# Six attention chunks, 32 feed-forward steps and all weight conversions of a fused kernel in one fixed order

## The chip, the cores and the metric

The kernel runs on one core of a Trainium2 chip, as one program. The metric is the device time of that program in microseconds (us). TensorE is written PE below, VectorE DVE, ScalarE ACT, GpSimd POOL, and SyncE, which starts the transfers, SP. A core has one queue of instructions for each engine; every queue runs in its own order, and an instruction that waits for another engine holds up all that stands behind it in its queue.

## What is computed

Three layers follow each other. The reference, cut to what matters:

```python
# attention: batch 2, heads 8, seq 768, head_dim 40, float32
for t in range(S):
    m_new = np.maximum(f_gate[:, :, t] + m, i_gate[:, :, t])
    f_stab = np.exp(f_gate[:, :, t] + m - m_new)
    i_stab = np.exp(i_gate[:, :, t] - m_new)
    m = m_new
    C = f_stab * C + i_stab * outer(vt, kt)
    n = f_stab * n + i_stab * kt
    y[:, :, t] = sigmoid(o_gate[:, :, t]) * (C @ qt) / max(|n . qt|, 1.0)
# feed-forward: 1536 tokens, d_model 320, d_ff 2048, weights in float64
h = x @ w_in
x = (np.maximum(0.01 * h, h) @ w_out).astype(np.float32)
# 8 experts, dense, d_ff 1024; P is a gate made doubly stochastic in 8 rounds
for e in range(E):
    out += P[:, e:e + 1] * (np.maximum(x @ w1[e], 0.0) @ w2[e])
```

The weights `w_in` and `w_out` are float64: a random float32 array times a float64 scale. The kernel gets them as raw 64-bit words and makes float32 out of them on the chip.

## The kernel before

**Numbers.** Every float32 factor of a large product is split into a high part, in the fp32r format that PE multiplies, and a low part, the residue. A product is then three passes: high by high, high by low, low by high.

**Attention.** The recurrence is worked in chunks of 128 positions of one batch, 12 in all (6 positions times 2 batches, `Chunk`). For a chunk PE makes the decay exponents from `stt` and `bd` (`decay`, L450; `bd` comes from `spread`, L441), ACT takes the exponential (L451) into `Dm`, POOL cuts it to the causal half with an affine_select (L452). PE makes the scores of the heads (`scores`, L460), DVE multiplies them with `Dm` into `Pm` (`weigh`, L466), POOL makes weighted keys `kw` (L473). PE multiplies `Pm` with the values (L478), recalls the state carried from earlier chunks (`zps`, L482) and makes the new state. DVE scales and adds (L496, L498), finds the denominator (L501 to L503), POOL multiplies the sigmoid gate with it (L507), DVE multiplies the result with that (L508). PE transposes it, ACT and DVE split it into the high and low input of the feed-forward layer, `xT` (`split_x`, L285 to L287). `gates` makes the running maxima and sums on DVE, and splits them.

**Feed-forward.** Tokens go in 6 blocks of 256, two chunks each; the 2048 hidden units go in 16 slices of 128. A step is one slice of one block, 96 in all. `up(g)` makes 8 matmuls of 128x256 (`mm1`, L165) into a PSUM bank `ha`, of which there are two; ACT applies the leaky ReLU from there into an SBUF tile `gg` (L558) and copies its high part `hha` (L561); the low part `hla` (L562) is a subtraction in POOL, and for the six steps in `V_STEPS` in DVE. `down(g)` adds 2 x 3 matmuls of 128x320 (`mm2`, L172 to L174) to the output banks `ya`, three steps after `up`. Steps run over block 0's first half, all of block 1, block 0's second half, and then block after block; block 0's two halves are added on DVE.

**Weights.** They come in 16 pieces, for each of 8 units one of `w_in` (768 columns in three rows of 256) and one of `w_out` (640). A piece is loaded on SP (`load`), ACT scales the upper word into a tile `up` and takes the top bits of the exponent (`prepare`, L127 and L130), DVE puts the sign in (L147) and joins the words to a float32 (L151), ACT copies the high part (L155), and POOL or, for the pieces of `V_PIECES`, DVE makes the low part (L156). Seven pieces of `HALVES` go through DVE in two halves.

**Order.** Up to the fourth piece chunks 0 and 1, the gates and the first conversions stand in an order written by hand (inside `tc.manual_schedule()`). After that the program is written step by step, with the rest hung ahead of and behind steps: `ATTEND` says at which steps the parts of a chunk come, `PIECES` at which steps a piece is converted. The framework's scheduler then places the instructions on the engines, by what is ready in its own estimate. Six chunks and all 16 pieces are placed by the time that step 32, the first of block 2, begins.

**Expert stage.** From 299.7 us on, eight experts run from their own hand-written order. It begins with the copies of its input, `X` (L222 to L229), which start during the last feed-forward steps.

## Time and profile before

| what | value |
|---|---|
| median of 3 runs | 968.94 us (968.02 to 975.64) |
| span of the profiled execution | 971.4 us |
| PE busy | 949.0 us, 98% |
| DVE busy | 575.3 us, 59% |
| ACT busy | 496.1 us, 51% |
| POOL busy | 608.8 us, 63% |
| start of the experts | 299.7 us |

Shares are averages over stages with different limits. The page's picture of the span in 40 slices, of 24.3 us each, shows where they differ: PE's row begins with 8 and 7 tenths and is then at 9 nearly throughout, and the clock that PE was granted is at 7, 5, 7, 9, 7 tenths in the first five slices and at 9 tenths or more behind them:

```
PE   8799999999999999999999999999999999999998
DVE  6769515142485658656666666566666666666655
ACT  5657444434466454555545455454454544545442
POOL 3354444644376656676777767777777677777762
PEclk7579799999999999999999999999999999999999
```

A busy PE at half clock does half the work of one at full clock, so both rows have to be read together.

### The profile page before, as it was taken

The page shows a single profiled execution, that of the slowest core. Times are in us where ns is not written, and L with a number is a line of the kernel's source. Part 1 is how long each engine was busy: PE and PEld are TensorE (multiplying, and loading weights), DVE is VectorE, ACT ScalarE, POOL GpSimd, SP SyncE. Part 2 cuts the span into 40 slices and gives each one's busy share as a digit, 9 for nine tenths or more (in the row PEclk, how much of TensorE's full clock was granted, in tenths as well). Part 3 has the DMA queues.
Part 4 walks back from the last instruction along what each step waited for, and adds up shares of the span by engine and source line. Part 5 has one row for each costly group of instructions (what it writes and reads, how often), then busy time and mean ns, then how long its engine had stood idle before and what let it go on. Part 6 is the DMA issues. An engine that isn't in the chain of part 4 may idle for free.

```text
span 971.4 us, 16851 instructions
## 1 busy us (share of the span) xinstructions
PE 949.0 (98%) x6174; PEld 920.4 (95%) x6174; DVE 575.3 (59%) x1121; ACT 496.1 (51%) x969; POOL 608.8 (63%) x618
## 2 busy tenths in 40 slices
PE   8799999999999999999999999999999999999998
PEld 6589898999989899999999999999999999999998
DVE  6769515142485658656666666566666666666655
ACT  5657444434466454555545455454454544545442
POOL 3354644444376656676777767777777677777762
PEclk7579799999999999999999999999999999999999
DMA  7545403010020111111111111111111111111102
GB/s 271 161 142 161 127 16 116 29 54 23 16 71 15 45 32 38 39 49 36 37 41 52 50 37 37 36 55 42 46 37 36 48 46 49 37 36 45 40 1 82
DMA packets 57161, 56.63 MB, mean 58 GB/s; under 512 B 7559, under 2 KB 47671, under 8 KB 57079
## 3 DMA queue, kind: packets, MB, share of 16 engines
q1 hardware_dynamic: 57078, 55.56, 18.8%
q8 instruction: 48, 0.79, 0.3%
q14 instruction: 35, 0.28, 0.1%
HBM read 53.57 MB, written 1.97 MB: 57 GB/s over the span
## 4 chain that ended last, share of the span: by engine, by line
PE 85%; DVE 4%; DMA 3%; ACT 2%; issue 2%; POOL 2%; SPq 1%; DVEq 0%; ACTq 0%; POOLq 0%
PE y L172 12%; PE y L173 11%; PE y L174 11%; PE b L881 8%; PE b L884 8%; PE b L882 8%; PE b L883 8%; PE ha L165 6%; PE ya L172 2%; PE yps L478 2%; PE ya L174 2%; DMA raw_a<-in_w_in_dram 2%; PE ya L173 2%; PE sps L460 1%; DMA R<-in_og_dram 1%
## 5 line engine op out<-in xcount | busy, mean ns | idle before, releaser
L903 POOL TENSOR_TENSOR hl<-c,hh 128x384 fp32r<-128x384 f32 x192 | 196.5, 1024 | 169.4 <-ACT c L902 148.2
L172 PE MATMUL y<-w_e,hh 128*128 128x320 f32 x768 | 238.1, 310 | 0.6 <-ACT acc L950 0.6
L173 PE MATMUL y<-w_e,hh 128*128 128x320 f32 x768 | 236.9, 308 | 0.0
L174 PE MATMUL y<-w_e,hl 128*128 128x320 f32 x768 | 236.8, 308 | 0.0
L954 DVE SCALAR_TENSOR_TENSOR acc<-y,Pg,acc 128x320 f32<-128x320 f32 x336 | 179.3, 548 | 63.4 <-PE y L174 56.3
L901 ACT ACTIVATE hh<-c 128x384 fp32r<-128x384 f32 x192 | 99.8, 520 | 207.4 <-DVE c L900 207.3
L881 PE MATMUL b<-X,w_e 128*128 128x384 f32 x448 | 152.9, 341 | 2.1 <-DVE s L912 1.5
L884 PE MATMUL b<-X,w_e 96*128 96x384 f32 x448 | 151.2, 337 | 0.0
L882 PE MATMUL b<-X,w_e 128*128 128x384 f32 x448 | 151.0, 337 | 0.0
L883 PE MATMUL b<-X,w_e 128*128 128x384 f32 x448 | 150.7, 336 | 0.0
L172 PEld LDWEIGHTS y<-w_e,hh 128*128 128x128 f32 x768 | 144.2, 188 | 1.9 <-ACT acc L950 1.0
L173 PEld LDWEIGHTS y<-w_e,hh 128*128 128x128 f32 x768 | 144.3, 188 | 0.0
L174 PEld LDWEIGHTS y<-w_e,hl 128*128 128x128 f32 x768 | 144.1, 188 | 0.0
L562 POOL TENSOR_TENSOR hla<-gg,hha 128x256 fp32r<-128x256 f32 x90 | 72.0, 802 | 96.9 <-ACT hha L561 84.5
L165 PE MATMUL ha<-xT,w_a 128*128 128x256 f32 x768 | 114.5, 292 | 3.7 <-ACT gg L558 2.5
L165 PEld LDWEIGHTS ha<-xT,w_a 128*128 128x128 f32 x768 | 103.4, 195 | 9.1 <-ACT gg L558 3.8
L902 ACT ACTIVATE c<-c 128x384 f32<-128x384 f32 x192 | 101.0, 526 | 17.8 <-ACT hh L901 0.7
L900 DVE TENSOR_TENSOR c<-b,s 128x384 f32<-128x384 f32 x192 | 100.7, 551 | 13.1 <-PE b L884 8.6
L919 DVE SCALAR_TENSOR_TENSOR hl<-b,hh 128x384 fp32r<-128x384 f32 x64 | 35.7, 558 | 94.7 <-ACT hh L918 94.6
L881 PEld LDWEIGHTS b<-X,w_e 128*128 128x128 f32 x448 | 84.8, 189 | 3.3 <-DVE s L912 2.2
L201 POOL TENSOR_TENSOR raw_e<-raw_e 128x256 f32<-128x256 f32 x116 | 84.4, 737 | 4.6
L882 PEld LDWEIGHTS b<-X,w_e 128*128 128x128 f32 x448 | 85.2, 190 | 0.0
(165 smaller groups left out, 1548.6 us busy)
## 6 DMA issues: line engine op xcount, KB each, us to landing
raw_e<-in_w_dram SPq DMA_DIRECT2D x32, 320.0 KB, 2.9
raw_e<-in_w_dram SPq DMA_DIRECT2D x62, 128.0 KB, 2.2
raw_e<-in_w_dram SPq DMA_DIRECT2D x248, 32.0 KB, 1.9
raw_a<-in_w_in_dram SPq DMA_DIRECT2D x8, 768.0 KB, 5.6
raw_a<-in_w_out_dram SPq DMA_DIRECT2D x8, 640.0 KB, 4.3
R<-in_kp_dram SPq DMA_DIRECT2D x11, 256.0 KB, 3.5
R<-in_qp_dram SPq DMA_DIRECT2D x11, 256.0 KB, 4.1
R<-in_vn_dram SPq DMA_DIRECT2D x11, 184.5 KB, 2.5
```

Of the source, the lines that this page charges most:

```text
L165: nc.tensor.matmul(h_ps, t1[:, ws, c * P:(c + 1) * P], xt[:, xs, t0:t0 + n], start=(j == 0), stop=(j == len(MM1) - 1),)
L172: nc.tensor.matmul(y_ps, a, t2[:, c, :], start=first, stop=False)
L173: nc.tensor.matmul(y_ps, a, t2[:, 2 + c, :], start=False, stop=False)
L174: nc.tensor.matmul(y_ps, b, t2[:, c, :], start=False, stop=last)
L881: nc.tensor.matmul(bank, f[:, 0], b[:, 0], start=fresh, stop=False, skip_group_check=not fresh)
L882: nc.tensor.matmul(bank, f[:, 0], b[:, 2], start=False, stop=False, skip_group_check=not fresh)
L883: nc.tensor.matmul(bank, f[:, 2], b[:, 0], start=False, stop=False, skip_group_check=not fresh)
L884: nc.tensor.matmul(bank, f[0:K3, 1], b[0:K3, 1], start=False, stop=True, skip_group_check=not fresh)
L900: nc.vector.tensor_tensor(c, part, plus, op=ALU.add)
L902: nc.scalar.activation(c, c, AF.Relu)
L903: nc.gpsimd.tensor_tensor(hl[a][b], c, hh[a][b].bitcast(F32), op=ALU.subtract)
L954: nc.vector.scalar_tensor_tensor(out=o, in0=y, scalar=Pg[:, 2 * HP * q + t, e:e + 1], in1=o, op0=ALU.mult, op1=ALU.add)
```

## The change

- **One table.** `ORDER` names everything that is done up to step 31's residue, in the order in which it is written to the queues, all inside `tc.manual_schedule()`: six chunks with their loads (`c0.kP` to `c5.xl`), the three parts of the gates (`a0` to `a8`, `n0` to `n8`, `f0` to `f8`), the 16 weight pieces (`L` load, `pu` scale, `pl` bits, `pa` sign, `pb` join, `ph` high, `px` low) and 32 feed-forward steps (`u` up, `g` leak, `h` high, `l` low, `d` down, `e` empty the output banks). `ATTEND`'s first rows, `PIECES`, `V_PIECES` and `V_STEPS` go.
- **Steps.** `RUNS` sets the first 32: block 0's slices 0 to 5, block 1's 0 to 9, block 0's 6 to 13, block 1's 10 to 15, block 0's 14 and 15. A block that is interrupted is summed through SBUF, so there are three such additions of two halves each, where there was one.
- **Leak in place.** `leak` writes the leaky values back into their PSUM bank, `inner_high` and `inner_low` read them there. `inner_low` is always on DVE. The tile `gg` is gone. This holds for all 96 steps.
- **Causal mask.** For chunks 0 to 3 a matmul of the identity with a mask of large negative numbers (bf16) adds the mask to the exponents in PSUM, two of 128x512 for a chunk; the affine_select is left for the later chunks.
- **Moved products.** In the table DVE makes the weighted keys, the gates with the denominator, the spreads and the weights' low parts, but for the eight in `POOLED`, which stay on POOL.
- **Weights.** No halves; the scale is written in place, so `up` goes, and its tile `rawU` becomes a fourth buffer of raw pieces.
- **Small things.** Reset flags and the mask are made by POOL's memsets at the start, the gates are loaded in three parts, the scores of chunks 0 and 1 use the feed-forward layer's banks, chunk 6 is loaded behind the table, its spread and one part of the decays come a little later.

From step 32 on the framework's scheduler places the instructions as before.

```diff
+RUNS = ((0, 0, 6), (1, 0, 10), (0, 6, 14), (1, 10, 16), (0, 14, 16))
+MASKED = (0, 1, 2, 3)
+POOLED = ('c0.kw', 'c1.kw', 'c4.kw', 'c4.sg', 'c5.sg', 'px14', 'px8', 'px9')
+ORDER = """
...
+px4 pl5 px3 pu6 L8 d0 c2.ya pu5 L7 c2.dn u2 c4.v pl6 c2.sg c2.ou c3.sc g2 c3.zt h2 pa5 l2 c2.tt pb5 u3 c2.xi c3.wg ph5
+u4 g3 px5 pu8 c3.va c2.xl g4 L9 pl8 pa6 h3 d1 c3.ya h4 pl7 c3.dn d2 l3 pu7 c3.sg u5 c3.ou pb6 c3.tt g5 c4.ap0 l4 c3.xi
...
-                self.up[p] = rawU[:, p * 3 * UW:p * 3 * UW + n]
-                nc.scalar.activation(self.up[p], self.raw[p][:, :, 1].bitcast(F32), AF.Copy, scale=F64_SCALE)
+                hw = self.raw[p][:, :, 1].bitcast(F32)
+                nc.scalar.activation(hw, hw, AF.Copy, scale=F64_SCALE)
...
+                nc.vector.scalar_tensor_tensor(out=hw, in0=hw, scalar=3, in1=lw, op0=ALU.logical_shift_left, op1=ALU.bitwise_or)
...
+        def low(self, p, eng):
+            t, n = self.t[p], (3, 2)[p]
+            eng.tensor_tensor(t[:, n:2 * n], self.value(p), t[:, 0:n].bitcast(F32), op=ALU.subtract)
...
+                nc.tensor.matmul(aps, stt[rs, s0:s0 + P], self.bd[rs, 4 * i:4 * i + 4, :], start=True, stop=not self.masked)
+                if self.masked:
+                    nc.tensor.matmul(aps, identb, mask.unsqueeze(1).to_broadcast([P, 4, P]), start=False, stop=True)
...
-            h_ps = ps_h.tile([P, BA], F32, tag="h", name=f"ha{g}")
-            mm1(h_ps, unitsA[f // 2].t[0], f % 2, xTb[j], 0, BA)
-            gg = ha.tile([P, BA], F32, tag="gg", name=f"gg{g}", bufs=4)
-            nc.scalar.activation(gg, h_ps, AF.Prelu, alpha=0.01)
+            h_ps[g] = ps_h.tile([P, BA], F32, tag="h", name=f"ha{g}")
+            mm1(h_ps[g], unitsA[f // 2].t[0], f % 2, xTb[j], 0, BA)
...
+        def leak(g):
+            nc.scalar.activation(h_ps[g], h_ps[g], AF.Prelu, alpha=0.01)
...
+        def inner_high(g):
             hh = ha.tile([P, BA], F32R, tag="hh", name=f"hha{g}")
             hl = ha.tile([P, BA], F32R, tag="hl", name=f"hla{g}")
-            nc.scalar.activation(hh, gg, AF.Copy)
-            (nc.vector if g in V_STEPS else nc.gpsimd).tensor_tensor(hl, gg, hh.bitcast(F32), op=ALU.subtract)
+            nc.scalar.activation(hh, h_ps[g], AF.Copy)
...
+        def inner_low(g):
+            hh, hl = hs[g]
+            nc.vector.tensor_tensor(hl, h_ps.pop(g), hh.bitcast(F32), op=ALU.subtract)
...
+        with tc.manual_schedule():
+            for name in ORDER.split():
+                tasks[name]()
+        chunks[6].load()
+        chunks[6].load_rest()
+        for g in range(TABLE, NG + LAG):
             if g < NG:
                 up(g)
+                leak(g)
+                inner_high(g)
+                inner_low(g)
             for fn in before[g]:
                 fn()
-            if g >= LAG:
-                down(g - LAG)
+            down(g - LAG)
+            empty(g - LAG)
```

Rows of the engines' queues follow, at three places: line, operation, target and sources (`w1` and `w2` are the converted pieces of a unit `a0` to `a7`, `raw` what they are made of, `R0` any of the chunks' tiles), and how many in a row.

First, DVE in the middle of the part. Before, between the residues of steps 14 and 15 and the scores of chunk 4 (`sps`):

```order
L562 TENSOR_TENSOR hla14_857<-gg14_854,hha14_856 128x256
L151 SCALAR_TENSOR_TENSOR raw0_a6_775<-rawU_94,raw0_a6_775 128x384 x2
L147 SCALAR_TENSOR_TENSOR raw1_a6_843<-raw1_a6_843 128x640
L562 TENSOR_TENSOR hla15_878<-gg15_875,hha15_877 128x256
L151 SCALAR_TENSOR_TENSOR raw1_a6_843<-rawU_94,raw1_a6_843 128x640
L156 TENSOR_TENSOR w1_a6_926<-raw0_a6_775,w1_a6_926 128x768
L147 SCALAR_TENSOR_TENSOR raw0_a7_894<-raw0_a7_894 128x768
L466 TENSOR_TENSOR R0_73<-sps0_4_971,R0_73 128x4x128
L466 TENSOR_TENSOR R0_73<-sps1_4_972,R0_73 128x4x128
L151 SCALAR_TENSOR_TENSOR raw0_a7_894<-rawU_94,raw0_a7_894 128x768
```

The same engine in the table, around the residues of steps 5 to 8:

```order
L667 TENSOR_TENSOR hla5_603<-ha5_562,hha5_602 128x256
L183 TENSOR_TENSOR w1_a3_592<-raw0_a3_354,w1_a3_592 128x768
L167 SCALAR_TENSOR_TENSOR raw0_a4_438<-raw0_a4_438 128x768
L161 SCALAR_TENSOR_TENSOR rawU_96<-rawU_96 128x640
L667 TENSOR_TENSOR hla6_634<-ha6_607,hha6_633 128x256
L167 SCALAR_TENSOR_TENSOR rawU_96<-rawU_96 128x640
L667 TENSOR_TENSOR hla7_661<-ha7_619,hha7_660 128x256
L548 TENSOR_TENSOR R0_75<-kn_3_330,Dm_3_349 128x320
L161 SCALAR_TENSOR_TENSOR raw1_a4_531<-raw1_a4_531 128x640
L183 TENSOR_TENSOR w2_a3_694<-rawU_96,w2_a3_694 128x640
L667 TENSOR_TENSOR hla8_705<-ha8_675,hha8_704 128x256
L167 SCALAR_TENSOR_TENSOR raw1_a4_531<-raw1_a4_531 128x640
```

Where two residues stood among runs of signs, joins and weight residues, each sign or join now has a residue of a step close by, read from the bank `ha`, and the conversions of units 3 and 4 fall to steps 5 to 8.

Second, PE where the first steps begin. Before, around steps 4 and 5, with the turning of the decays (`dps128`, `dpc`) in between:

```order
L165 MATMUL ha4_476<-xT0_286,w1_a2_333 128x256 x4
L388 MATMUL dps128_454<-cst_70,sc1_93 128x64 x2
L165 MATMUL ha4_476<-xT0_286,w1_a2_333 128x256
L165 MATMUL ha5_555<-xT0_286,w1_a2_333 128x256 x2
L165 MATMUL ha4_476<-xT0_286,w1_a2_333 128x256
L394 MATMUL dpc128_0_458<-sc1_93,sc0_92 120x2 x3
L165 MATMUL ha4_476<-xT0_286,w1_a2_333 128x256 x2
L165 MATMUL ha5_555<-xT0_286,w1_a2_333 128x256 x6
L174 MATMUL ya0_0_0_468<-w2_a1_313,hla2_420 128x320
L174 MATMUL ya0_0_1_469<-w2_a1_313,hla2_420 128x320
L394 MATMUL dpc128_1_463<-sc1_93,sc0_92 120x2 x3
```

In the table, around steps 3 and 4, with the values of chunk 3 (`yps_3`):

```order
L191 MATMUL ha3_491<-xT0_290,w1_a1_302 128x256 x8
L191 MATMUL ha4_507<-xT0_290,w1_a2_418 128x256 x8
L553 MATMUL yps_3_519<-vt_3_351,Pm_3_502 128x41 x8
L198 MATMUL ya0_0_0_440<-w2_a0_314,hha1_411 128x320
L199 MATMUL ya0_0_0_440<-w2_a0_314,hha1_411 128x320
L200 MATMUL ya0_0_0_440<-w2_a0_314,hla1_412 128x320
L198 MATMUL ya0_0_1_441<-w2_a0_314,hha1_411 128x320
L199 MATMUL ya0_0_1_441<-w2_a0_314,hha1_411 128x320
L200 MATMUL ya0_0_1_441<-w2_a0_314,hla1_412 128x320
```

Before, the matmuls of two steps were mixed with each other and with small ones of the decays; now whole steps follow each other, with whole parts of chunks between them, and chunk 3 is at its values as step 4 ends.

Third, DVE at the end of the feed-forward layer, where the copies for the expert stage (`X0`) begin. Before:

```order
L286 TENSOR_TENSOR xT5_2815<-pt_a10_2810,xT5_2815 64x128
L287 TENSOR_TENSOR xT5_2815<-pt_a10_2810,xT5_2815 128x2x128
L286 TENSOR_TENSOR xT5_2815<-pt_a11_2819,xT5_2815 64x128
L287 TENSOR_TENSOR xT5_2815<-pt_a11_2819,xT5_2815 128x2x128
L225 TENSOR_TENSOR X0_2854<-rawx_0_0_1529,X0_2854 128x4x128
L229 TENSOR_TENSOR X0_2854<-rawx_0_0_1529,X0_2854 32x4x128
L225 TENSOR_TENSOR X0_2854<-rawx_0_0_1529,X0_2854 128x3x128
L229 TENSOR_TENSOR X0_2854<-rawx_0_0_1529,X0_2854 32x3x128
L225 TENSOR_TENSOR X0_2854<-rawx_0_1_2108,X0_2854 128x4x128
```

And after, behind the residue of step 78:

```order
L667 TENSOR_TENSOR hla78_2739<-ha78_2728,hha78_2738 128x256
L314 TENSOR_TENSOR xT5_2747<-pt_a10_2742,xT5_2747 64x128
L315 TENSOR_TENSOR xT5_2747<-pt_a10_2742,xT5_2747 128x2x128
L314 TENSOR_TENSOR xT5_2747<-pt_a11_2751,xT5_2747 64x128
L315 TENSOR_TENSOR xT5_2747<-pt_a11_2751,xT5_2747 128x2x128
L251 TENSOR_TENSOR X0_2785<-rawx_0_0_1503,X0_2785 128x4x128
L255 TENSOR_TENSOR X0_2785<-rawx_0_0_1503,X0_2785 32x4x128
L251 TENSOR_TENSOR X0_2785<-rawx_0_0_1503,X0_2785 128x3x128
L255 TENSOR_TENSOR X0_2785<-rawx_0_0_1503,X0_2785 32x3x128
L251 TENSOR_TENSOR X0_2785<-rawx_0_1_2064,X0_2785 128x4x128
L667 TENSOR_TENSOR hla79_2776<-ha79_2765,hha79_2775 128x256
```

The copies are the same, but DVE's queue now also holds the residues of all steps, and nine operations stand between that of step 78 and that of step 79.

## Rows read from the trace of the kernel before

**Rows 1.** Stretches: PE, PEld, DVE, ACT, POOL busy us (count), PE clock, DMA share, GB/s

```profile
14.20:38.10 23.90, 19.41 (x84) 17.58 (x84) 18.30 (x33) 15.08 (x22) 11.79 (x8) 0.50 0.62 210
...
65.40:109.80 44.40, 41.72 (x321) 38.50 (x320) 36.15 (x61) 32.32 (x67) 20.72 (x18) 1.00 0.54 174
...
139.40:264.30 124.90, 123.69 (x986) 118.45 (x985) 39.82 (x97) 56.36 (x129) 52.72 (x66) 1.00 0.15 46
```

**Rows 2.** Stretches, same columns: the whole part up to step 32

```profile
0.00:139.40 139.40, 125.49 (x767) 110.00 (x768) 90.80 (x165) 81.02 (x157) 62.44 (x59) 0.82 0.47 153
```

**Rows 3.** Timeline of PE: start us, duration us, engine, line, operation, count

```profile
1.38 7.43 PE L708 MATMUL warm<-R 128*128 128x512 bf16 x20 [1.38 <-DVE wgr L82]
...
85.35 1.12 PE L165 MATMUL ha<-xT,w_a 128*128 128x256 f32 x8
86.30 0.31 PE L172 MATMUL ya<-w_a,hha 128*128 128x320 f32 x1
...
87.18 1.12 PE L165 MATMUL ha<-xT,w_a 128*128 128x256 f32 x8
...
139.43 1.11 PE L165 MATMUL ha<-xT,w_a 128*128 128x256 f32 x8
```

**Rows 4.** VectorE's groups to 139.4: busy us, mean ns | idle before, releaser

```profile
L151 DVE SCALAR_TENSOR_TENSOR raw_a<-rawU,raw_a 128x320 int32<-128x320 int32 (+3 forms) x23 | 21.0, 941 | 0.1
L147 DVE SCALAR_TENSOR_TENSOR raw_a<-raw_a 128x320 int32<-128x320 int32 (+3 forms) x23 | 17.8, 797 | 8.1 <-ACT raw_a L130 7.4 <-issue 0.7
L156 DVE TENSOR_TENSOR w_a<-raw_a,w_a 128x640 fp32r<-128x640 f32 (+1 forms) x8 | 8.0, 996 | 2.7 <-ACT w_a L155 2.7
...
L562 DVE TENSOR_TENSOR hla<-gg,hha 128x256 fp32r<-128x256 f32 x6 | 3.4, 570 | 0.4 <-ACT hha L561 0.4
...
L287 DVE TENSOR_TENSOR xT<-pt_a,xT 128x256 fp32r<-128x256 f32 x6 | 2.5, 425 | 0.1
...
L508 DVE TENSOR_TENSOR R<-R 128x320 f32<-128x320 f32 x4 | 1.9, 486 | 0.6 <-POOL R L507 0.6
...
L441 DVE TENSOR_TENSOR bd<-mv,cst 64x1024 fp32r<-64x1024 f32 x1 | 1.2, 1209 | 0.0
...
L82 DVE MEMSET wgr<- 128x32 f32 x1 | 0.1, 85 | 0.0
```

**Rows 5.** The same view with shapes kept apart, to 137 us

```profile
L151 DVE SCALAR_TENSOR_TENSOR raw_a<-rawU,raw_a 128x768 int32<-128x768 int32 x5 | 4.8, 951 | 0.0
```

**Rows 6.** VectorE's waits from 65.4 to 109.8: us in total, times, longest

```profile
DVE raw_a L147 <- ACT raw_a L130: 3.6, 1, 3.6
```

**Rows 7.** Timeline of VectorE, columns as in rows 3

```profile
3.27 0.42 DVE L359 TENSOR_TENSOR_SCAN sc<-sc 64x128 f32<-64x128 f32 x1 [1.91 <-DMA sc<-in_gates_dram]
...
46.90 4.97 DVE L151 SCALAR_TENSOR_TENSOR raw_a<-rawU,raw_a 128x384 int32<-128x384 int32 x4
...
96.64 0.81 DVE L151 SCALAR_TENSOR_TENSOR raw_a<-rawU,raw_a 128x640 int32<-128x640 int32 x1
97.38 0.94 DVE L156 TENSOR_TENSOR w_a<-raw_a,w_a 128x768 fp32r<-128x768 f32 x1
```

**Rows 8.** GpSimd's groups to 139.4, columns as in rows 4

```profile
L562 POOL TENSOR_TENSOR hla<-gg,hha 128x256 fp32r<-128x256 f32 x25 | 22.2, 889 | 34.6 <-ACT hha L561 31.9 <-issue 2.7
L156 POOL TENSOR_TENSOR w_a<-raw_a,w_a 128x768 fp32r<-128x768 f32 (+1 forms) x8 | 15.7, 1964 | 8.6 <-ACT w_a L155 8.5
L452 POOL TENSOR_SCALAR_AFFINE_SELECT R<-R 128x1024 f32<-128x1024 f32 x5 | 7.2, 1436 | 11.8 <-ACT R L451 10.6 <-issue 1.2
...
L507 POOL TENSOR_TENSOR R<-R,den 128x320 f32<-128x320 f32 x6 | 4.9, 824 | 13.3 <-DVE den L503 13.3
```

**Rows 9.** Timeline of GpSimd, columns as in rows 3

```profile
49.39 2.13 POOL L441 TENSOR_TENSOR bd<-mv,cst 64x1024 fp32r<-64x1024 f32 x1
```

**Rows 10.** Timeline of ScalarE, columns as in rows 3

```profile
264.43 1.07 ACT L222 ACTIVATE X<-rawx 128x1024 fp32r<-128x1024 f32 x1
265.38 0.43 ACT L561 ACTIVATE hha<-gg 128x256 fp32r<-128x256 f32 x1
```

More of the change, by code (lines that the diff above doesn't have):

```diff
@@ new lines, in gates, with decays_turn @@
+            (split_m, mix_m), (split_s, mix_s) = halves(mv, Gt, Ft, 0), halves(stt, It, T1, 3)
+            return [maxima, starts, totals, decay, growth, split_m, split_s, mix_m, mix_s]
+        def decays_turn(a, z):
+            c0, c1 = a // P, z // P
+            dps = decay_banks[a] = ps_b.tile([P, 512], F32, tag="b1", name=f"dps{a}")
+            for c in range(c0, c1):
+                nc.tensor.transpose(dps[:, (c - c0) * R:(c - c0 + 1) * R], Gt[:, c * P:(c + 1) * P], ident[0:R, 0:R])
@@ L762, in mlstm_moe_kernel, with constants @@
-        step_piece(4)
-        c2.load_rest()
-        step_piece(5)
-        for g in range(NG + LAG):
+        nc.gpsimd.memset(rst, 1.0)
+        nc.gpsimd.memset(rst.rearrange("r (c t) -> r c t", t=P)[:, :, 0], 0.0)
+        causal = places["Pm"][:, 0, :]
+        nc.gpsimd.memset(causal, 0.0)
+        nc.gpsimd.affine_select(out=causal, in_=causal, pattern=[[1, P]], compare_op=ALU.is_ge, fill=NEG, base=0, channel_multiplier=-1)
+        nc.gpsimd.memset(kw[:, 8, :], 0.0)
+        def constants():
+            nc.sync.dma_start(cst, cst_in)
+            nc.vector.tensor_copy(mask, causal)
+            nc.scalar.activation(identb, ident, AF.Copy)
@@ new lines, in mlstm_moe_kernel @@
+        for c in chunks[0:6]:
+            chunk_tasks(c)
+        for n in range(2 * NUA):
+            u, p = unitsA[n // 2], n % 2
+            for k, fn in (("L", u.load), ("pu", u.scale), ("pl", u.bits), ("pa", u.sign), ("pb", u.join), ("ph", u.high)):
+                tasks[f"{k}{n}"] = lambda fn=fn, p=p: fn(p)
+            tasks[f"px{n}"] = lambda u=u, p=p, n=n: u.low(p, engine(f"px{n}"))
+        for g in range(TABLE):
+            for k, fn in (("u", up), ("g", leak), ("h", inner_high), ("l", inner_low), ("d", down), ("e", empty)):
+                tasks[f"{k}{g}"] = lambda fn=fn, g=g: fn(g)
```

463 lines of the change are left out of this document (228 added, 235 removed).

## The prediction

> **What bounds the kernel now.** I read the split of the span into stretches first, by the clock that TensorE was granted [rows 1], then TensorE's timeline in the middle [rows 3], then VectorE's groups up to the end of the part that the table replaces [rows 4, 5]. The part ends with the start of up step 32, the first matmul of block 2. Before the change it stands at 139.43 us [rows 3]. What follows is TensorE's: from 139.4 to 264.3 PE is busy 123.69 of 124.90 us [rows 1], so a microsecond won ahead of step 32 is a microsecond of the kernel, unless the later code loses it again.
>
> Ahead of 139.4 PE is busy 125.49 us, at a mean clock of 0.82 [rows 2]: 13.9 us are idle, and the clock costs 0.18 x 139.4 = 25.1 us. At full clock one up step follows the other after 87.18 - 85.35 = 1.83 us, its down step included [rows 3]. The stretch from 139.4 to 264.3 holds 48 steps, 87.8 us, and six chunks: 124.9 - 87.8 - 1.2 idle = 35.9 us, 6.0 a chunk. Chunks 0 and 1 recall no state, so I give the first six 33 us. With the warming matmuls (to 1.38 + 7.43 = 8.8 us [rows 3]) and 31 pitches (56.7) PE's own work ahead of step 32 is 98.5 us at full clock. It takes 139.4: about 41 us are to be had there, and no more.
>
> Who keeps PE from it? VectorE is busy 90.80 of 139.4 us, ScalarE 81.02, GpSimd 62.44 [rows 2]. No engine is full, but all four have similar work in one chain of weight conversions, and between 65.4 and 109.8 VectorE is busy 36.15 of 44.40 us, a fill of 0.81 [rows 1]; 3.6 us of what is missing are a single wait for ScalarE's bits [rows 6]. The part is thus bound by the order of work on VectorE and ScalarE, with the lost clock on top.
>
> **The change on PE.** It adds the masks, 8 matmuls of 128x512 in bf16. Such a one takes 7.43/20 = 0.37 us [rows 3], so 3.0 us, and PE's work becomes 101.5 us. The first long half-clock stretch, 14.2 to 38.1, falls while weights are still being loaded and converted; I keep its loss of half of 23.9, 12 us [rows 1]. PE could then reach step 32 at 113.5 at the earliest.
>
> **The change on VectorE** is the term that decides, since step 32 needs the low part of block 2's input, which is VectorE's last work in the table. All durations of its groups up to 139.4 add up to 97.1 us (36 groups, the first and the last in [rows 4]); they fill only 90.80 us because one operation starts a little before the last one's end: the residue at 97.38 by 0.07 us, since 96.64 + 0.81 = 97.45 [rows 7]. The ratio is 0.935.
> - Out: the joins 21.0, the signs 17.8, the weight residues 8.0 and six inner residues 3.4 [rows 4], which leaves 46.9.
> - Conversions come back in whole pieces, 8 of 768 columns and 8 of 640, a sign and a join each. A join of 768 took 0.95 [rows 5], one of 640 0.81 [rows 7]; signs I take like joins: 16 x 0.95 + 16 x 0.81 = 28.2.
> - Weight residues, 13 of 16 (three stay on GpSimd): 6 x 0.94 and 7 x 0.81, those of 640 columns priced like a join of that shape [rows 7]: 11.3.
> - Inner residues, all 32, out of PSUM. The nearest row with a PSUM source and 128x256 elements took 0.425, the form with both sources in SBUF 0.570 [rows 4]. I take 0.43, 13.8 in all; with the other form it would be 18.2.
> - From GpSimd: two spreads of 1.21, three weighings of keys and four gates at 0.49 [rows 4], two sums of partial outputs at the same price, and the mask's cast, an estimated 0.2: 7.0.
>
> That is 46.9 + 28.2 + 11.3 + 13.8 + 7.0 = 107.2 us of durations.
>
> **GpSimd beside it.** What stays there in the table is 3 x 0.82 + 2 x 1.44 + 3 x 1.96 + 2 x 0.82 = 12.9 us (weighings and gates priced as L507, the masks of chunks 4 and 5, three weight residues [rows 8]). VectorE pays for company: four halved joins took 4.97 us from 46.90 on [rows 7], where half pieces at half of 0.95 and 0.81 would take about 1.8; GpSimd's spread of 2.13 us lay inside [rows 9]. Over the whole part the blocked price is lower: joins and signs took 38.8 us in place of the 28.2 of the whole pieces above, 10.6 us (the fixed cost of the halves included) beside 62.44 us of GpSimd, 0.17 for each. I add 0.17 x 12.9 = 2.2; the bounds are 0 and 12.9. The Trainium skill, *SBUF — State Buffer*, section *Who interferes with whom*, has a stricter rule: a VectorE instruction with two SBUF inputs and a GpSimd instruction that reads SBUF exclude each other, and the later one blocks entirely. The trace agrees that such joins suffer, and that the PSUM-sourced form does not (mean 0.425 over six); whether for GpSimd's whole length, no row tells; by the rule the sum would take 12.9 in place of 2.2, which is rival C's first half.
>
> So 109.4 us of durations, 102.3 of busy time after the ratio 0.935. The order fills VectorE's queue by hand and puts inner residues between conversions, where before whole runs of conversions stood (the first order rows). I take a fill of 0.83: above the 0.81 of the best stretch, below the 36.15/(44.4 - 3.6) = 0.89 that it would have without its one long wait, as scaling and bits now stand earlier in ScalarE's queue. VectorE begins at 3.27 [rows 7]: 3.3 + 102.3/0.83 = **126.5 us for step 32, 12.9 earlier**. ScalarE's operations stay nearly the same, 81 us [rows 2], and it has room.
>
> **After the table.** The up matmul's bank is now held until VectorE's residue has read it, where it was free after ScalarE's leak. The high part takes 0.43 [rows 10]; the leak priced like it, the low part at 0.43 and three handovers of an estimated 0.1 make 1.6 us. The bank is wanted again by the second next up step, 2 x 1.83 - (86.30 - 85.35) = 2.7 us after [rows 3]. That covers it while neither queue is late. It is late where chunk work or the copies of the expert stage's inputs stand ahead: ScalarE's copy at 264.43 takes 1.07 [rows 10], and five VectorE copies now stand between two residues (the last order rows). GpSimd's residues, and their 0.89 us each [rows 8], leave the chain in return. I take 2 us of loss over 64 steps; the bounds are 0 and 6. The expert stage is the same code with the same engine as its bound and I cost it at nothing.
>
> The profiled span is 971.4 us, 2.5 above the median of the runs; differences are taken over to the median. 968.9 - 12.9 + 2 = **958.0 us**.
>
> **Rivals.**
> - **B, the table packs better**: PE's own limit. Step 32 at 113.5 means 25.9 us won, less 2: 945 us. It needs a VectorE fill of 0.93; the best seen is 0.81 over 44 us. For it: PE's idle time falls and half-clock stretches, which came after idle time, may vanish with it. Chance 0.16 for under 948.
> - **C, VectorE pays more than I reckon**: blocked for all of GpSimd's 12.9 us, it has (107.2 + 12.9) x 0.935/0.83 = 135.3, step 32 at 138.6, and the kernel 970.1. Or PE falls to half clock once more: a stretch like the one of 23.9 us costs 12. 964 to 978.6, chance 0.21.
> - **D, the other side: VectorE becomes the bound.** If it fills no better than in the whole part before, 90.8/(139.4 - 3.3) = 0.667, step 32 comes at 3.3 + 153.4 = 156.7 and the kernel at 988.2. It decides below a fill of 0.76, where nothing is won, and below 0.71 it costs more than 1%. For it: VectorE takes 45 residues where it took 14, and the moved products on top, and every inner residue now keeps an up bank. Against it: in the best stretch nearly half of the idle 8.3 us was one wait [rows 1, 6]. Chance 0.17.
> - That the change does nothing is the case of a fill near 0.76, inside C.
>
> **How the numbers follow.** My forecast, 948 to 964, has 0.46. A measurement of this kernel tells about 1% from no change, so faster means under 959.3 and slower over 978.6. Faster: B's 0.16 and 0.34 of the forecast's 0.46, together 0.50. Within 1%: the other 0.12 and C's 0.21, 0.33. Slower: D, 0.17. The range reaches from 944, below which some 0.06 lie, to 980, above which 0.14 of D lies; it holds cases of both signs, and the likeliest one's own range is 948 to 964.
>
> **What would show it.** Step 32 near 127 us, and VectorE's busy share to there near 0.83; a share below 0.76 is D. The inner residue near 0.43 us, sign and join at 0.95 and 0.81; means 15% above that are C. From step 32 to step 80 the distance stays within 2 us of 124.9; waits of up steps for VectorE's residues would show the held bank. If step 32 comes early and the end does not, the held bank has eaten it; if it comes late with VectorE idle, the order itself has put someone behind a late transfer.

## The result

The changed kernel takes 956.59 us in the median of four runs (954.29 to 956.99), the kernel before 970.29 us (968.02 to 975.64). The ratio is 0.9847 with a 95% interval from 0.9815 to 0.9879: 1.5% faster, 11.7 to 17.9 us. A second set of runs, beside the experiments, gave 0.9825 (0.9797 to 0.9852). The forecast was 958.0 us. Two later runs, one of 4029.93 us at a mean granted clock of 0.216 and one of 1011.2 us at 0.839, lie far off the others of their kernels and are left out of all figures below.

The two profiled executions stand further apart than the medians (13.7 us): 971.4 us before, 952.5 after, 18.9 us less. The time of a run is about 2 us longer than its span in the profile (954.29 with 952.5), so the profiled execution of the kernel before stands some 3 us above its median, and the one of the changed kernel 2.3 below. The profiled run of the changed kernel is the fastest of its four, with a mean granted clock of 0.989; the other three have 0.986 and 0.987, and 0.002 to 0.003 of 953 us are 2 to 3 us. So where a run's time is compared with another's below, a difference of 2 us may be the clock, and the place in the trace says more than the time.

### The profile page after: what moved, and what is told of

Read it like the earlier page. It is cut to its first block, busy times and chain, and to the rows that moved or that the text cites. A ratio compares the mean times of both kernels' runs of the same rounds, so it can differ in the third digit from the quotient of the medians.

```text
span 952.5 us, 16825 instructions
## 1 busy us (share of the span) xinstructions
PE 935.6 (98%) x6182; PEld 908.0 (95%) x6182; DVE 601.4 (63%) x1216; ACT 495.8 (52%) x972; POOL 515.4 (54%) x514
## 4 chain that ended last, share of the span: by engine, by line
PE 88%; DVE 6%; DMA 3%; ACT 2%; issue 1%; SPq 1%; DVEq 0%; ACTq 0%
PE y L198 12%; PE y L199 12%; PE y L200 12%; PE ha L191 8%; PE b L949 8%; PE b L952 8%; PE b L950 8%; PE b L951 8%; PE ya L198 2%; PE ya L200 2%; PE ya L199 2%; PE yps L553 1%; DMA raw_a<-in_w_out_dram 1%; PE sps L537 1%; PE zps L559 1%
## 5 line engine op out<-in xcount | busy, mean ns | idle before, releaser
L191 PE MATMUL ha<-xT,w_a 128*128 128x256 f32 x768 | 109.4, 287 | 4.4 <-DVE hla L667 4.2
L191 PEld LDWEIGHTS ha<-xT,w_a 128*128 128x128 f32 x768 | 99.7, 191 | 8.9 <-DVE hla L667 8.0
L952 PEld LDWEIGHTS b<-X,w_e 96*128 96x128 f32 x448 | 84.2, 188 | 0.5 <-POOL X L255 0.5
```

The costliest lines, as they stand in the source:

```text
L191: nc.tensor.matmul(h_ps, t1[:, ws, c * P:(c + 1) * P], xt[:, xs, t0:t0 + n], start=(j == 0), stop=(j == len(MM1) - 1),)
L952: nc.tensor.matmul(bank, f[0:K3, 1], b[0:K3, 1], start=False, stop=True, skip_group_check=not fresh)
```

## The profile after

The stretches of the changed kernel, with the columns of [rows 1]: first the part up to step 32, which now begins at 117.0 us (139.4 before), then the 48 steps behind it, then the last 16 up to the first expert.

```profile
0.00:117.00 117.00, 110.27 (x765) 96.51 (x765) 101.03 (x191) 83.03 (x157) 17.16 (x20) 0.91 0.56 181
...
117.00:243.60 126.60, 125.26 (x995) 119.52 (x996) 56.31 (x151) 54.52 (x132) 17.59 (x18) 1.00 0.15 46
243.60:280.60 37.00, 34.34 (x251) 32.81 (x251) 24.90 (x47) 22.63 (x50) 10.31 (x7) 1.00 0.20 56
280.60:952.50 671.90, 665.75 (x4175) 659.12 (x4173) 419.21 (x829) 335.66 (x636) 470.31 (x469) 1.00 0.14 41
```

Against [rows 2] the first part lost 22.4 us. VectorE is busy 101.03 us in place of 90.80, GpSimd 17.16 in place of 62.44, and the mean clock is 0.91 in place of 0.82. The 48 steps take 126.6 us where they took 124.9 [rows 1]; the last stretch takes 37.0 where it took 35.4 (264.3 to 299.7). The experts take 671.9 us, as before (671.7).

The same first part of the changed kernel by the clock:

```profile
0.00:14.90 14.90, 11.58 (x62) 5.53 (x63) 6.95 (x18) 6.49 (x13) 1.26 (x9) 1.00 0.83 259
14.90:35.40 20.50, 19.32 (x75) 15.71 (x76) 19.65 (x34) 18.06 (x26) 1.47 (x2) 0.50 0.99 311
35.40:117.00 81.60, 79.38 (x630) 75.27 (x629) 74.43 (x141) 58.48 (x120) 14.43 (x9) 1.00 0.40 134
```

One early stretch at half clock is left, and from 35.4 us on the clock is full. It pays to look at the time from the first up step to step 32 alone, in the kernel before and in the changed one:

```profile
31.90:139.40 107.50, 100.48 (x654) 92.29 (x654) 68.35 (x125) 64.92 (x132) 50.11 (x45) 0.84 0.39 125
```
```profile
33.00:117.00 84.00, 81.78 (x641) 77.67 (x640) 76.80 (x144) 60.85 (x123) 14.43 (x9) 0.99 0.42 140
```

Before, four stretches of this part ran at half clock:

```profile
31.90:38.10 6.20, 6.20 (x27) 5.37 (x26) 3.52 (x8) 4.73 (x7) 2.10 (x1) 0.50 0.40 134
41.50:48.30 6.80, 6.03 (x19) 4.59 (x19) 4.67 (x9) 6.71 (x12) 2.03 (x3) 0.50 0.30 103
55.20:65.40 10.20, 10.20 (x52) 9.63 (x53) 3.73 (x8) 6.28 (x15) 5.84 (x5) 0.50 0.35 136
109.80:120.00 10.20, 10.20 (x53) 9.76 (x53) 6.26 (x16) 0.48 (x2) 5.86 (x7) 0.50 0.38 116
```

Half of TensorE's 32.6 busy us in them, 16.3, is lost to the clock, which leaves 84.2 us of work at full speed; after, only 33.0 to 35.4 is at half clock, 1.2 us are lost, and 80.6 us are work. So the 23.5 us between 107.5 and 84.0 are about 15.1 us of lost clock, 4.8 us of idle time (7.0 less 2.2), and 3.6 us of work, of which about 1 us are decays that now lie behind the table. In this account of TensorE's time, from one profile of each kernel, two thirds of what was won is clock.

TensorE's timeline in that part, only rows with a wait, shows how clock and waits go together. Before:

```profile
41.79 1.43 PE L165 MATMUL ha<-xT,w_a 128*128 128x256 f32 x5 [1.40 <-ACT gg L558]
...
52.53 0.33 PE L388 MATMUL dps<-cst,sc 64*128 64x64 f32 x2 [1.95 <-DVE R L466]
...
104.14 1.22 PE L165 MATMUL ha<-xT,w_a 128*128 128x256 f32 x8 [0.86 <-ACT gg L558]
108.54 0.62 PE L165 MATMUL ha<-xT,w_a 128*128 128x256 f32 x3 [0.85 <-DVE w_a L156]
```

And after, all waits of the matmuls that it shows from 45 to 117 us:

```profile
45.93 0.44 PE L305 MATMUL pt_a<-cst,R 128*128 128x128 f32 x2 [0.50 <-DVE R L570]
48.93 1.75 PE L553 MATMUL yps<-vt,Pm 128*128 128x41 f32 x14 [0.18 <-DVE Pm L543]
96.33 1.21 PE L191 MATMUL ha<-xT,w_a 128*128 128x256 f32 x8 [0.43 <-DVE hla L667]
```

Before, waits of 0.85 to 1.95 us stand at or ahead of the start of the last three half-clock stretches. After, no wait from 45 us on is longer than half a microsecond, and the clock stays full. That the waits bring the half clock is read from this order alone, and not each wait does: one of 0.66 us at 83.3 in the kernel before, and one of 1.69 us at 40.1 in a run below (the products back on GpSimd), had none behind them for 26 and 97 us.

VectorE's groups of the changed kernel up to step 32, shapes kept apart, columns as in [rows 4]:

```profile
L667 DVE TENSOR_TENSOR hla<-ha,hha 128x256 fp32r<-128x256 f32 x32 | 13.0, 413 | 3.4 <-ACT hha L662 3.4
L161 DVE SCALAR_TENSOR_TENSOR raw_a<-raw_a 128x768 int32<-128x768 int32 x8 | 8.9, 1112 | 0.3 <-ACT raw_a L149 0.3
L167 DVE SCALAR_TENSOR_TENSOR raw_a<-raw_a 128x768 int32<-128x768 int32 x8 | 7.6, 955 | 0.1
...
L167 DVE SCALAR_TENSOR_TENSOR rawU<-rawU 128x640 int32<-128x640 int32 x4 | 4.6, 1151 | 0.0
```

The residue out of PSUM takes 0.413 us (0.43 was taken), the unblocked join of 768 columns 0.955 (0.95 was taken); two of the groups shown, at 1112 and 1151 ns, are longer than their shape asks for. In each it is one operation held up beside GpSimd; at 60.30, for example, a join of 640 columns takes 2.16 us.

## The experiments

What has to be told apart: does VectorE's queue set the end of the table, as the prediction has it, or TensorE's own work, or the chain through ScalarE? Which part of the change wins: the order, the leak in PSUM with the cheap residue, or the products moved off GpSimd? And what does the held bank cost behind the table?

### More work on one engine at a time

Three runs, profiled once each, add about the same work to each of the 32 steps of the table, on VectorE, on ScalarE, on TensorE.

```diff
 def inner_low(g):
     nc.vector.tensor_tensor(hl, h_ps.pop(g), hh.bitcast(F32), op=ALU.subtract)
+    if g < TABLE:
+        nc.vector.tensor_tensor(idle[1], idle[0], idle[0], op=ALU.subtract)
```

> The changed kernel with one more VectorE operation of 128x256 (scratch tile to scratch tile, about 0.41 us) behind each inner residue of the table's 32 steps: 13 us of durations, about 12 us of busy time more on VectorE. Theory (VectorE's queue sets when the table ends; it is busy 101 of the 117 us to step 32): step 32 starts 9 to 12 us later, at 126 to 129. Rival 1 (TensorE's own work sets it, it is busy 110 of 117): under 5 us later, since VectorE has 16 us of room. Rival 2 (the chain through ScalarE sets it): 0 to 3 us later.

```diff
 def inner_high(g):
     nc.scalar.activation(hh, h_ps[g], AF.Copy)
+    if g < TABLE:
+        nc.scalar.activation(idle[1], idle[0], AF.Copy)
```

> The changed kernel with one more ScalarE copy of 128x256 (scratch to scratch, about 0.42 us) behind each high copy of the table's 32 steps: 13.4 us more on ScalarE, which is busy 83 of 117. Theory (VectorE's queue): step 32 at 117 to 121. Rival 1 (TensorE's own work): 117 to 119. Rival 2 (the chain through ScalarE): 126 or later.

```diff
 def up(g):
+    if g < TABLE:
+        for k, (ws, xs) in enumerate(MM1[0:3]):
+            nc.tensor.matmul(h_ps[g], ...same weights and input..., start=(k == 0), stop=(k == 2))
     mm1(h_ps[g], unitsA[f // 2].t[0], f % 2, xTb[j], 0, BA)
```

> The changed kernel with the first three of the eight up matmuls done twice in the table's 32 steps: 96 matmuls of 0.12 us, 11.4 us more on TensorE. Theory (VectorE's queue): TensorE has 6.7 us of idle time to 117 and takes part of it up: step 32 at 121 to 125, idle time to there under 4 us. Rival 1 (TensorE's own work sets the end): the whole 11.4 us, step 32 at 128 or later, idle time unchanged.

Step 32 came at 125.2, 122.7 and 126.0 us: 8.2, 5.7 and 9.0 later than in the changed kernel. None of these lies in a range that the theory or a rival had named: 125.2 lies between the theory's 126 and the first rival's 122, 122.7 above the theory's 121 and below the second rival's 126, 126.0 between the theory's 125 and the rival's 128. But the clock differs. The stretch from the first up step to step 32 in each, with VectorE's, ScalarE's and TensorE's addition in this order:

```profile
32.50:125.20 92.70, 85.90 (x640) 79.78 (x640) 86.80 (x177) 61.29 (x123) 16.12 (x9) 0.96 0.39 129
```
```profile
33.00:122.70 89.70, 85.70 (x644) 81.26 (x642) 77.23 (x146) 70.08 (x155) 14.13 (x9) 0.94 0.41 134
```
```profile
33.10:126.00 92.90, 91.51 (x735) 87.90 (x735) 77.77 (x145) 62.07 (x123) 13.97 (x9) 1.00 0.40 129
```

The first two fell to half clock once more:

```profile
41.70:48.50 6.80, 6.80 (x34) 6.58 (x35) 4.38 (x13) 2.92 (x5) 0.00 (x0) 0.50 0.78 267
```
```profile
39.70:50.00 10.30, 9.40 (x46) 9.21 (x48) 6.53 (x16) 6.23 (x12) 0.00 (x0) 0.50 0.67 232
```

Half of 6.8 and of 10.3 us taken off, the stretches are 89.3, 84.6 and 92.9 us, against 84.0 less the 1.2 us that the changed kernel loses to its clock, that is 82.8. (Four profiles of the same table, the changed kernel's two and the two with another leak behind the table, lie between 82.8 and 83.9, so these differences hold to about 1 us.) So 10.0 us more of VectorE's busy time cost 6.5 us, 9.2 more of ScalarE's 1.8, and 10.9 more of TensorE's work (91.5 against 80.6) 10.1. ScalarE is nearly out. TensorE's own work is the first bound, at nearly one for one, and its idle time falls from 2.2 to 1.4 us; VectorE stands close behind it, at about two thirds. The rival's expectation for TensorE, idle time unchanged, was not met either: 0.8 us of it were filled.

### One part alone: leak in PSUM and residues on VectorE

The kernel before, its order, conversions and products left as they were:

```diff
-            gg = ha.tile([P, BA], F32, tag="gg", name=f"gg{g}", bufs=4)
-            nc.scalar.activation(gg, h_ps, AF.Prelu, alpha=0.01)
-            nc.scalar.activation(hh, gg, AF.Copy)
-            (nc.vector if g in V_STEPS else nc.gpsimd).tensor_tensor(hl, gg, hh.bitcast(F32), op=ALU.subtract)
+            nc.scalar.activation(h_ps, h_ps, AF.Prelu, alpha=0.01)
+            nc.scalar.activation(hh, h_ps, AF.Copy)
+            nc.vector.tensor_tensor(hl, h_ps, hh.bitcast(F32), op=ALU.subtract)
```

> The kernel before with one part of the change alone: leak in place in the PSUM bank, and all inner residues on VectorE out of PSUM, in all 96 steps; the order by step lists and the scheduler, the weights and all other products as before. Theory (the fixed order is what wins, since it fills VectorE's queue without gaps): no gain, 966 to 976 us, step 32 at 136 to 144. Rival (the cheaper residue, 0.43 us in place of 0.89 on GpSimd, and the quieter GpSimd are what wins): 955 to 962 us, step 32 before 130.

971.45 us; the ratio to the kernel before is 1.0013 (0.9986 to 1.0041): no difference. In the trace step 32 comes at 133.4 us, 6.0 earlier, and behind it a part of the time is given back:

```profile
31.40:133.40 102.00, 95.09 (x654) 87.42 (x654) 71.45 (x150) 64.64 (x132) 27.29 (x20) 0.88 0.41 132
...
133.40:258.90 125.50, 123.96 (x987) 118.53 (x986) 54.78 (x146) 54.31 (x130) 17.62 (x18) 1.00 0.16 46
258.90:295.90 37.00, 34.32 (x251) 32.79 (x251) 24.94 (x47) 22.64 (x50) 10.33 (x7) 1.00 0.20 56
```

From the first up step to step 32 TensorE is idle for 6.9 us, as before (7.0), and does the same work; of the 5.5 us that this stretch is shorter, about 5 are lost clock. Behind step 32, 0.6 and 1.6 us are given back (125.5 and 37.0 us in place of 124.9 and 35.4). The 3.9 us that remain between the two spans, 971.4 and 967.5, are no gain of the kernel: the profiled run here is 2.0 us below the median of its kernel, and that of the kernel before some 2 us above. The expected no-gain is right, step 32 came a little ahead of its range. The mean clock up to step 32 is 0.83 and VectorE is busy 93.88 of 133.4 us: without the table, the stalls and the half clock stay.

### One part undone: the products back on GpSimd

```diff
-POOLED = ('c0.kw', 'c1.kw', 'c4.kw', 'c4.sg', 'c5.sg', 'px14', 'px8', 'px9')
+POOLED = (all of kw and sg of chunks 0 to 5, 'c2.bd', 'c4.bd', 'px0', 'px1', 'px2', 'px4', 'px6', 'px8', 'px13', 'px15')
```

> The changed kernel with its order kept and the moved products taken back to GpSimd: all weighings and gates of the table, the spreads for chunks 2 to 5, and the weight residues that the kernel before had there (pieces 0, 1, 2, 4, 6, 8, 13, 15). VectorE loses about 10 us of its own work, GpSimd gains about 20. Theory (VectorE's busy time sets the table's end, at two thirds of what is added or taken): less 10, plus 3 to 5 of blocking, step 32 at 112 to 115. Rival (a product on GpSimd takes twice as long and stands in the chain of a chunk or a weight piece, with VectorE's ordered queue held behind it): first up step 1.5 to 4 us later, VectorE's busy share to step 32 under 0.80 in place of 0.86, step 32 at 120 to 132.

956.16 us, ratio 0.9827 (0.9805 to 0.9849), as the changed kernel. Step 32 comes at 117.7 us; the first up step at 34.0, 1.0 later. The part up to step 32:

```profile
0.00:117.70 117.70, 110.26 (x765) 96.82 (x766) 94.97 (x177) 83.29 (x157) 35.41 (x34) 0.90 0.56 180
```

VectorE is busy 6.1 us less and GpSimd 18 us more, and the time is the same. Both expectations are wrong: VectorE's relief brings nothing, as fits a table bound by TensorE, and GpSimd's slower products, with VectorE waiting 3.1 us for its gates and TensorE 1.7 for a product, cost little. That the two do not merely cancel is not shown by this run alone. So "VectorE takes most of GpSimd's early products" is not what wins. The other way round:

```diff
-POOLED = ('c0.kw', 'c1.kw', 'c4.kw', 'c4.sg', 'c5.sg', 'px14', 'px8', 'px9')
+POOLED = ()
```

> The changed kernel with the list of products that stay on GpSimd emptied: three weighings, two gates and three weight residues, 5.1 us at the prices of the trace, go to VectorE too; only the causal masks of chunks 4 and 5 stay on GpSimd in the table. Theory (VectorE's queue sets the end at about two thirds, as 8.2 us for 12 more showed): step 32 later by 2 to 4 us, less what VectorE gains from a quiet GpSimd. Rival C of the prediction (VectorE is blocked for the whole of GpSimd's work): the joins and residues beside GpSimd shorten by some 10 us in sum and step 32 comes earlier.

Step 32 at 118.9 us, 1.9 later, in a single run. (The kernel's 959.12 us hold a half-clock stretch at 136.9 to 143.7, behind the table, that the changed kernel's profile lacks.) VectorE's busy time up to there is 100.95 us, no more than the 101.03 of the changed kernel, though eight operations of 5.1 us were added:

```profile
0.00:118.90 118.90, 111.42 (x766) 95.41 (x766) 100.95 (x199) 83.20 (x157) 7.38 (x12) 0.91 0.56 178
```

Its groups that were long above:

```profile
L161 DVE SCALAR_TENSOR_TENSOR raw_a<-raw_a 128x768 int32<-128x768 int32 x8 | 7.6, 950 | 0.0
...
L167 DVE SCALAR_TENSOR_TENSOR rawU<-rawU 128x640 int32<-128x640 int32 x4 | 3.3, 813 | 0.0
```

1112 ns became 950, 1151 became 813. The durations of VectorE's operations add up to 0.8 us more than in the changed kernel, so those that were there before are 4.3 us shorter: the 17.16 - 7.38 = 9.8 us that left GpSimd had cost VectorE 4.3 us of blocking, 0.44 for each. That is under half of what the rival named, and the end did not come earlier; why it came 1.9 us later, with VectorE no busier, is not settled. What stays on GpSimd blocks VectorE in both runs. In the changed kernel a sign of 640 columns, 0.82 us elsewhere, takes 1.71 beside the mask of chunk 4:

```profile
58.33 1.71 DVE L161 SCALAR_TENSOR_TENSOR rawU<-rawU 128x640 int32<-128x640 int32 x1
```
```profile
57.65 1.72 POOL L521 TENSOR_SCALAR_AFFINE_SELECT R<-R 128x1024 f32<-128x1024 f32 x1 [28.92 <-ACT R L518]
```

Together with an operation held up beside the mask of chunk 5 (at 83.35) and one beside a spread (at 100.60) this is about 3.5 us more.

### One part undone: the causal mask

```diff
-MASKED = (0, 1, 2, 3)
+MASKED = ()
 (and c0.af to c3.af, the affine_select, in the order behind each chunk's second exponential)
```

> The changed kernel with the causal mask of chunks 0 to 3 taken back to GpSimd's affine_select behind the exponential; the 8 mask matmuls go. TensorE has 2.5 to 3 us less, GpSimd 4 x 1.2 to 1.4 us more, and the scores wait 1.2 to 1.4 us longer for chunks 0 and 1. Theory (TensorE and VectorE both near their limit in the table): nearly even, step 32 at 115.5 to 118.5. Rival (the early chain through chunks 0 and 1 sets the first step): first up step 1.5 us or more later, and step 32 with it, 118.5 to 121.

963.75 us, a single run. Step 32 came at 122.1 us, 5.1 later; the first up step at 34.8, 1.8 later. TensorE's early wait:

```profile
PE dps L419 <- issue: 4.9, 1, 4.9
```

In the changed kernel the same instruction waited 1.7 us, in its repeat 0.6. Behind it stand two half-clock stretches, and a third of 10.2 us behind the table, at 139.7:

```profile
13.40:37.30 23.90, 18.34 (x74) 15.80 (x75) 23.00 (x38) 20.27 (x29) 5.31 (x5) 0.50 0.88 276
40.70:50.90 10.20, 10.03 (x44) 9.54 (x46) 8.31 (x17) 4.67 (x7) 0.84 (x1) 0.50 0.73 243
```

Together the two are 13.6 us longer than the changed kernel's one, 6.8 us of lost clock. From the first up step to step 32 it is 87.3 us; less 6.3 of lost clock that is 81.0, below the changed kernel's 82.8, which fits the mask's matmuls being gone. So the rival of the expectation, the early chain, holds for the first step, which comes 1.8 us later; the other 3.3 of the 5.1 us are no more than clock. Whether the half clock at 40.7 belongs to the kernel or to this one run is not shown, as the clock falls differently from run to run; without it the mask in PSUM would by this account be worth little.

### One part undone: the leak in PSUM

Behind the table only (with VectorE, then with GpSimd making the residue), then in all steps:

```diff
 def leak(g):
-    nc.scalar.activation(h_ps[g], h_ps[g], AF.Prelu, alpha=0.01)
+    h = h_ps[g]
+    if g >= TABLE:
+        h_ps[g] = ha.tile([P, BA], F32, tag="gg", name=f"gg{g}", bufs=4)
+    nc.scalar.activation(h_ps[g], h, AF.Prelu, alpha=0.01)
```

> The changed kernel with one part undone behind the table: in steps 32 to 95 the leaky values go to an SBUF tile as before the change, and VectorE takes the residue from there; the up bank is free after the leak. Theory (the held bank costs what is lost after the table): the distance from step 80 to step 95 falls from 32.5 to about 31 us, step 32 to 80 by about 1 us, 2 us in all. Rival (the loss comes from work that moved behind the table, the decays and chunk 6's loads): both distances stay within 0.5 us, the time too.

> As the run before, with the residues of steps 32 to 95 on GpSimd: steps behind the table as they were before the change. Theory (held bank): the same 2 us won, or a little less, as a GpSimd residue takes 0.89 us. Rival 1 (VectorE's queue, not the bank, is late at the end of the layer): it wins more than the run with VectorE, by 1 us or more. Rival 2 (moved work): no change within 0.5 us.

> The changed kernel with the leak put back into an SBUF tile in all 96 steps, the residue on VectorE from there. Theory (the bank is held too long only where VectorE's queue is late, behind the table): step 32 within 1 us of 116.8, the kernel within 2 us of the run that does this behind the table alone (950.5). Rival (the held bank slows the table's steps too): step 32 at 114 to 115.5. Second rival (a residue with both sources in SBUF is slowed by GpSimd): mean residue in the table over 0.50 us, step 32 at 118 to 120.

The changed kernel ran beside the first two:

> The changed kernel itself, once more, as the measure for the two that follow: 955 to 958 us, step 32 at 117 to 120.

It took 954.06 us (ratio 0.9825, 0.9797 to 0.9852). With the SBUF tile behind the table the kernel takes **950.53 us, ratio 0.9771 (0.9750 to 0.9793)**, which beats both kernels, the changed one narrowly; with it in all steps 950.84 us, ratio 0.9784 (0.9755 to 0.9813), no different; with GpSimd's residues 955.46 us, ratio 0.9825 (0.9802 to 0.9848).

Behind the table, the changed kernel's repeat and then the run with the tile:

```profile
117.30:243.30 126.00, 125.21 (x995) 119.45 (x996) 56.83 (x150) 54.47 (x132) 17.59 (x18) 1.00 0.15 46
243.30:280.30 37.00, 34.34 (x251) 32.81 (x251) 24.92 (x47) 22.70 (x50) 10.58 (x7) 1.00 0.20 56
```
```profile
116.80:242.00 125.20, 124.55 (x994) 119.11 (x995) 58.62 (x149) 56.70 (x131) 17.79 (x18) 1.00 0.15 46
242.00:276.00 34.00, 33.71 (x253) 32.95 (x252) 27.72 (x48) 22.93 (x50) 10.22 (x7) 1.00 0.22 61
```

From step 80 to step 95 it is 29.5 us in place of 32.6 (1.5 expected, 3.1 measured), from step 32 to 80 0.8 us less: 3.9 us for the held bank. (The spans, 952.2 and 947.8 us, are 4.4 apart; the other 0.5 stands ahead of step 32, where both run the same program.) TensorE's waits in the last stretch, changed kernel and then the run with the tile:

```profile
PE ha L191 <- DVE hla L667: 2.6, 3, 1.1
```
```profile
PE ya L200 <- DVE hla L670: 0.3, 1, 0.3
```

And VectorE in the changed kernel where it is late; the residue at 245.99 stands behind two copies of the experts' input, and the up matmuls at 246.46 start only when it is done:

```profile
244.80 0.55 DVE L255 TENSOR_TENSOR X<-rawx,X 32x384 fp32r<-32x384 f32 x1
245.38 0.69 DVE L251 TENSOR_TENSOR X<-rawx,X 128x512 fp32r<-128x512 f32 x1
245.99 0.42 DVE L667 TENSOR_TENSOR hla<-ha,hha 128x256 fp32r<-128x256 f32 x1
```
```profile
246.46 1.20 PE L191 MATMUL ha<-xT,w_a 128*128 128x256 f32 x8 [0.61 <-DVE hla L667]
```

The run with GpSimd has 30.9 us from step 80 to 95, as the kernel before, 1.7 less than the changed kernel; it also fell to half clock from 143.9 to 150.7, which costs 3.4 us, so its time says less than this distance. The theory of the held bank is shown, and it is twice as large as expected; both rivals of it fall, the second (moved work) by this distance and not by the time with GpSimd. In the table no price of the bank is visible: with the tile in all steps step 32 comes at 116.4 in place of 116.8, as near as two runs of one program stand, and the residue takes 0.467 us in place of 0.413.

### What the early half clock costs

```diff
+        def fill(n):
+            extra = ps_y.tile([P, 512], F32, tag="ya0", name="extra")
+            for _ in range(n):
+                nc.tensor.matmul(extra, zero[:, 0:P], zero[:, 0:512], start=True, stop=True)
 (in the order: 4 ahead of c1.sc, 4 to 6 each behind c0.va, c1.va, c0.tt, c2.ap0, c2.ap1, c3.ap1, c1.tt)
```

> The run with the leak in SBUF behind the table, with 36 idle matmuls of 128x512 (bf16, on zeros, results unused) put between TensorE's work from about 11 to 33 us, so that it has nearly no idle time there. It asks what the early stretch at half clock (17.0 to 34.0 in that run) costs. Theory (VectorE's queue, 95% busy from 14 us on, sets the pace there): whether the clock stays full or not, step 32 comes within 2 us of 116.8. Rival (the lost clock is lost time): if the half-clock stretch goes or shrinks to under 8 us, step 32 comes 4 to 8 us earlier, the kernel at 943 to 947. If the stretch stays, step 32 moves by the added matmuls, up to 8 us later, and the question stays open.

953.89 us, ratio 0.9805 (0.9773 to 0.9837); the kernel without the filling, the one with the SBUF tile behind the table, took 950.53. The stretch at half clock shrank from 17.1 to 6.8 us (15.1 to 21.9), yet the first up step came at 34.1 us in place of 33.0. From 20 to 50 us, in tens:

```profile
20.00:30.00 10.00, 10.00 (x52) 5.88 (x51) 9.33 (x20) 9.12 (x15) 0.00 (x0) 0.90 1.00 297
30.00:40.00 10.00, 9.11 (x67) 6.81 (x66) 9.16 (x14) 8.15 (x12) 0.74 (x1) 1.00 0.68 218
40.00:50.00 10.00, 7.89 (x39) 7.73 (x40) 6.18 (x16) 5.19 (x9) 0.00 (x0) 0.66 0.68 227
```

Up to 42 us TensorE had its full clock back and nothing came of it, since VectorE is busy 9.3 of 10 us there and its weight residue at 41.60 stands 1 us later than in the run without the filling (40.63). The filling takes TensorE's time itself, so this run alone does not prove that the early clock is not lost time. The other runs say it more cleanly, as eight profiles run the same program up to the first up step (two of them with one more memset). Their early half clock lasts 13.7 us in one (VectorE's addition, first up step at 32.5), 17.1 in two (SBUF tile behind the table, residues on VectorE and on GpSimd: 33.0 and 32.7), and 20.5 in five (32.2 to 33.4). Up to 3.4 us less of lost clock bring the first step no earlier than it also comes with the longest stretch: there, with VectorE busy 19.65 of 20.50 us in the changed kernel's early stretch, no cost of the early clock is visible. At 40 us TensorE then waited 2.1 us, fell to half clock at 42.4, and VectorE waited 3.6 us for it; step 32 came at 121.5, which neither expectation had. Why the recall at 40 us waited was not settled.

## Why the prediction came out

The time, 958.0 against 956.6, is right, and it is right by luck more than by its mechanism. Step 32 came 9.5 us earlier than forecast and the loss behind the table was 1.3 us larger, which would put the forecast about 8 us too high; but the traces overstate the gain by 5.2 us (18.9 against 13.7 between the medians), and the median before rose by 1.4 us with a fourth run.

- **VectorE's sum**: 102.3 us of busy time forecast, 101.03 measured. The prices read from rows for single operations held (0.43 and 0.413 for the residue, 0.95 and 0.955 for the join). The sum held because two terms missed in opposite directions: the blocking beside GpSimd is about 7.8 us where 2.2 were taken (below), and VectorE's own work is about 101 us where 107.2 were taken (its groups add up to 108.8, counted as the prediction counts them, less the 7.8). Besides, the 97.1 us of the groups are busy times; the durations add up to 99.0, so the ratio was 0.917 and not 0.935.
- **The step that failed: "the term that decides", with a fill of 0.83.** The measured fill is 101.03/(117.0 - 3.3) = 0.89, and step 32 came at 117.0, not at 126.5. The fill was taken from the kernel before, as if VectorE's queue alone set the end. It does not: 10 us added to VectorE cost 6.5, taking 6.1 us off it brought nothing, and TensorE answers to added work at nearly one for one. The first bound was TensorE's own work, which the prediction had nearly right (98.5 and 3.0 us; 110.27 less half of the 19.32 busy at half clock, 100.6, measured), and named as rival B with 113.5 us. The rest to 117.0 is 9.7 us of lost clock, 12 were taken, and 6.7 us of idle time, which that rival left out.
- **The clock** was kept out of the forecast but for 12 us early on. Measured are 10.2 us up to step 32, after 25 before. Most of the gain is there by TensorE's account, as the later half-clock stretches are gone; "half-clock stretches may vanish with it" stood in rival B alone.
- **After the table**: 2 us of loss were taken, 0 to 6 as bounds; measured are 1.6 us from step 32 to 80 and 1.7 to step 95, 3.3 together. The place (the copies for the experts) was right. The bank alone costs 3.9; a part of this VectorE's residues give back, which from SBUF are faster than GpSimd's (29.5 against 30.9 us for the last steps).
- **GpSimd beside VectorE**: 2.2 us were taken for 12.9 us, at 0.17 for each; the run with an emptied list shows 4.3 us for 9.8, 0.44 for each, and about 3.5 us stand beside the masks and a spread that it left. The rule of the Trainium skill, *SBUF — State Buffer*, *Who interferes with whom*, that the later of the two blocks entirely, would by an estimate make it up to the whole 9.8; the measured price lies between the two. Single operations in the trace agree with the rule: when the sign at 58.33 starts, 1.04 us of GpSimd's mask are left, and it takes 0.9 us longer than elsewhere. The trace also agrees that residues out of PSUM, with one SBUF input, are spared: 0.413 us with GpSimd busy 17 us, and 0.414 with 35.
- **Rival D** did not occur: VectorE's fill stayed above 0.76 in every run of the changed kernel. **Rival C's** further half-clock stretches did occur in some experiments, and cost 1.7 to 5.1 us each.

What is left as the winner is the order: the same 32 steps and six chunks, laid so that TensorE no longer waits in the middle. The leak in PSUM alone wins nothing, and undoing it behind the table wins 3.9 us more; the moved products win nothing. This is an argument by elimination. The order was not run by itself, and the whole pieces, the scale in place and the fourth raw buffer were not undone one by one. Whether the mask in PSUM belongs to the gain with more than the 1.8 us of the first step is open.
